# Four of twelve heads' score moves issued by GpSimd from the fourth chunk on

## The chip, the cores and the metric

The kernel runs on one core of one Trainium2 chip. That core has five engines that work side by side, each on its own list of instructions in a fixed order: TensorE (PE in the profile, with its weight loads as PEld), VectorE (DVE), ScalarE (ACT), GpSimd (POOL) and SyncE (SP). An instruction that has to wait holds up all that stand behind it on its engine. DMAs are issued by an instruction of SyncE, GpSimd or ScalarE and then move data on their own. The metric is the device time of one execution in microseconds; the median of several executions is compared.

## The reference

Attention with four batches, twelve heads, 448 rows and 64 columns per head, in which the scores of the twelve heads are mixed with one another before the softmax and once more after it; then two dense layers with an ELU between them; then two dense layers with a softmax gate and a layer norm between them.

```
scores = scale * np.matmul(q, k.transpose(0, 1, 3, 2))
scores = np.einsum('bhij,hg->bgij', scores, w_pre)
scores = scores - np.max(scores, axis=-1, keepdims=True)
attn = np.exp(scores)
attn = attn / (np.sum(attn, axis=-1, keepdims=True) + 1e-09)
attn = np.einsum('bhij,hg->bgij', attn, w_post)
return np.matmul(attn, v).astype(np.float32)          # -> x, 1792 x 768
...
h = x @ w_in                                          # 768 -> 2048
g = np.where(h > 0.0, h, alpha * (np.exp(np.minimum(h, 0.0)) - 1.0))
return (g @ w_out).astype(np.float32)                 # 2048 -> 768
...
h = x @ w_in                                          # 768 -> 1024
sm = e / (np.sum(e, axis=-1, keepdims=True) + 1e-09)
solu = h * sm
ln = (solu - mu) / np.sqrt(var + 1e-06) * g_ln
return (ln @ w_out).astype(np.float32)                # 1024 -> 768
```

## The kernel before

**Attention** is cut into 17 chunks of query rows (numbered 0 to 16), counted in groups of ten rows: 4, 8, 12, 12 and 9 groups in the first batch, 12, 12, 12 and 9 in the others. Two neighbouring groups make a unit (the last of a nine-group chunk has one group), numbered through all chunks; units 88 to 92 lie in the last chunk, among the first work of the dense layers.

For each chunk, `add_score` makes the raw scores: q and k tiles are multiplied two heads at a time on TensorE into PSUM (`sc`, line 445), and ScalarE or VectorE copies each head's scores into one of eight SBUF buffers `sev` (`evac`, line 451). In `sev` a partition is a query row. The mix over heads contracts over the head index, so heads and rows have to stand on the partitions together: a DMA per head, the *move* (`move`, issued through the helper `dma`, line 402), spreads the rows of `sev` into the tile `sp` at a stride of thirteen partitions. A chunk has thirteen moves, one for each of heads 0 to 10 and two half ones for head 11. There are two `sp` tiles, used in turn by the chunks.

When all thirteen moves of a chunk have landed, its units can be mixed: `pm` (line 515) is four matmuls by `w_pre` for each of the unit's groups, the maxima (`st`, line 520) are on VectorE, the exponentials with their sums (`e`, line 525) on ScalarE, then two small operations on VectorE (lines 529 and 532) give the reciprocals. `wr` (line 536, on GpSimd mostly, else on VectorE) multiplies them into the weights of the second mix, which is `po` (line 548): 32 matmuls for each group, with `e` as the stationary operand, so the scores come out transposed. `at` (line 556) copies them to SBUF, `av` (line 597) multiplies by v, `x` (line 604) copies out of PSUM, and a store puts it in DRAM as `xs`. The score making of chunk c + 1 goes between the units of chunk c. In the background the weights of the first dense layers, which arrive as float64 bits, are decoded (`kst`, lines 635 to 652, stored as `w1s`).

At the **handover** to the dense layers, the loads of x (`xst`, line 221, from `xs`), their split into a high and a low fp32r part (cast `xh`, line 225, and subtraction `xl`, line 230) and the split of the first weights (`wy`, lines 693 and 696) stand on the same engines as the last chunk's units. After it come the dense layers (`h`, line 258, and on).

**What sets the order.** Every step of attention is an `op` with a rank (the time it is wanted), the steps it depends on, the buffers it takes and frees, and the engines that may run it with a cost in microseconds on each: `act=.54, dve=.62` lets the planner choose between ScalarE and VectorE. `schedule` goes through the ops in order of time: for each engine it takes the ready op that can start first, keeps that engine's clock, and writes the instruction out. So the costs and the engines of one op change the planned times of all that follow, and with them the order on every engine. A move is planned to land 3.5 us after its end (`lag=3.5`). On the chip the planned times play no part; only the order on each engine and the waits between them stay.

In the kernel before, a move costs .78 on SyncE, may also go to ScalarE in chunks 0 and 1 (`act=.78`), and to GpSimd in chunks 1 and 2 (`pool=1.1`). From chunk 3 on all moves are SyncE's, which also issues the loads of q, k and v, the stores of `xs`, the traffic of the weight decoding and the loads of x.

Of the kernel before, what the change touches and what calls it, by code (L numbers as in the profile page):

```python
# [64 lines left out]
def kernel(ctx: ExitStack, tc: tile.TileContext, qa, kt, vt, wpre, wpost,  # L65
# [223 lines left out]
    def op(rank, emit, deps=(), new=(), uses=(), more=0.0, lag=None, **us):  # L289

        o = Op()
        o.rank, o.emit, o.deps, o.new, o.us, o.more, o.lag = rank, emit, [d for d in deps if d is not None], new, us, more, lag
        for b in chain(new, uses):
            b.users.append(o)
        ops.append(o)
        return o
# [61 lines left out]
    def copier(e):  # L358
        return nc.scalar.copy if e == "act" else nc.vector.tensor_copy
# [15 lines left out]
    for u in range(NU):  # L375
# [4 lines left out]
        c = units[u][0]  # L380
        n = u - first[c]
# [15 lines left out]
    kt_t, kb, q_t, qb_, sp_t, sp_op, pre_op, e_t = {}, {}, {}, {}, {}, {}, {}, {}  # L397
# [3 lines left out]
    def dma(out, in_, e="sp"):  # L401
        {"act": nc.scalar, "pool": nc.gpsimd, "sp": nc.sync}[e].dma_start(out=out, in_=in_)
# [27 lines left out]
    def add_score(c, h):  # L430

        b, _, G = CH[c]
        n = 5 * G
        ring = ("sc", "po", "pm")[h // 2 % 3] if c == 0 else "sc"
        scb, svb = [Buf(ring) for _ in range(2)], [Buf("sev") for _ in range(2)]
        r = t_sc[c, h]
        key = "sc", c, h

        def mm(e):
            T[key] = [pools["ps_" + ring].tile([128, 512], F32, tag=ring, name="sc") for _ in range(2)]  # L440
            q, k = q_t[c, h // 6], kt_t[b, h]
            for x in range(2):
                for i in range(2):
                    sl = slice(64 * i, 64 * i + 64)
                    nc.tensor.matmul(T[key][i][64 * x:64 * x + 64, :S], q[sl, h % 6 // 2, 64 * x:64 * x + 64], k[sl, :],  # L445
                                     start=True, stop=True)

        def evac(e, i):
            t = T["sv", c, h + i] = (k0.tile([128, S], F32, name=f"s0_{h + i}") if c == 0 else
                                     sev_p.tile([128, S], F32, tag="sev", name="sev"))  # L450
            copier(e)(t, T[key][i][:, :S])

        def move(e, i, p, r0, r1):
            if c not in sp_t:
                sp_t[c] = sp_t[c - 2]
            dma(sp_t[c][p:p + 13 * (r1 - r0 - 1) + 1:13, 0:G, :], T["sv", c, h + i][r0 * G:r1 * G], e)

        o1 = op(r, mm, [k_op[b, h], q_op[c, h // 6]], scb, [qb_[c, h // 6], kb[b, h]], pe=SC)
        for i in range(2):
            sv = [] if c == 0 else [svb[i]]  # L460
            o2 = sc_ev[c, h + i] = op(r + .9 + .1 * i, lambda e, i=i: evac(e, i), [o1], sv, [scb[i]], act=.54, dve=.62)
            for n, to in enumerate([(h + i, 0, 10)] if h + i < 11 else [(11, 0, 5), (64, 5, 10)]):
                sp_op.setdefault(c, []).append(op(r + 2 + .2 * i + .1 * n, lambda e, i=i, to=to: move(e, i, *to), [o2], [spb_[c]], sv, lag=3.5, sp=.78, **({"act": .78} if c < 2 else {}), **({"pool": 1.1} if 0 < c < 3 else {})))

    spb_ = {c: Buf(f"sp{(NC - c) % 2}") for c in range(NC)}
    o = op(7.0, lambda e: dma(wpre_t, wpre), sp=.5)
# [18 lines left out]
    for c in range(NC):  # L485
        b = CH[c][0]
        if c == HEAD[b]:
            for h in range(0, NH, 2):
                add_k(b, h)
        for hf in range(2):  # L490
            add_q(c, hf)
        for h in range(0, NH, 2):
            add_score(c, h)
# [81 lines left out]
    for c in range(NC):  # L575
# [12 lines left out]
        for n in range(2):  # L588
            r = t_av[c, n]
# [388 lines left out]
```

## Time and profile before

| | us |
|---|---|
| median of 3 runs | 1119.38 |
| lowest, highest | 1118.16, 1119.91 |
| profiled execution | 1116.97 |
| its span, first to last instruction | 1115.2 |

Its mean granted clock of TensorE is 0.992 of the full one. Busy shares of the span: TensorE 96% (1075.3 us), VectorE 65%, ScalarE 45%, GpSimd 22%. The rows come from one profiled execution, from whose start all times are counted. A matmul count stands for single instructions. "[0.88 <-DMA xs<-x]" says that the engine sat idle for 0.88 us just before, and what ended that by the trace: where a wait is for several DMAs, the one named is not always the one meant. SPq is the queue of DMA issues on SyncE; the duration there is that of the issuing, not of the transfer.

### The profile page before, as it was taken

How to read it: one execution, taken by the hardware profiler on the slowest of the kernel's cores; microseconds unless marked ns; L12 is line 12 of the kernel's file. 1: busy time of each engine (PE TensorE's matmuls, PEld its weight loads, DVE VectorE, ACT ScalarE, POOL GpSimd, SP SyncE). 2: the span in 40 equal slices, each digit the busy share in tenths (PEclk: the TensorE clock that was granted, in tenths of full speed). 3: DMA queues.
4: the chain of work that ended last, by engine and by line, in shares of the span. 5: the costliest groups of instructions: out<-in, count | busy, mean ns of one | idle time of the engine just before them, and what ended most of it. 6: DMA issues, size and time to landing. Idle time of an engine off the chain costs nothing. (4 is left out here: it accounts for less than half of the span.)

```text
span 1115.2 us, 29836 instructions
## 1 busy us (share of the span) xinstructions
PE 1075.3 (96%) x12520; PEld 903.6 (81%) x12520; DVE 727.4 (65%) x1404; ACT 502.5 (45%) x1069; POOL 241.3 (22%) x249
## 2 busy tenths in 40 slices
PE   7889999999998899999999999999999999999998
PEld 2557677667665798898988999999989899898988
DVE  5577677777676647688878887878854553443532
ACT  3466666666665445433333343333431343333422
POOL 3111001011012323444434434343422000000000
PEclk9999999999999899999999999999999999999999
DMA  7775775775744334142434242324162600000001
GB/s 220 192 216 157 227 214 180 229 215 171 219 146 159 119 98 132 63 145 95 170 95 162 84 138 88 127 67 157 30 218 103 245 29 15 29 15 29 22 22 43
DMA packets 80315, 141.76 MB, mean 127 GB/s; under 512 B 20847, under 2 KB 60003, under 8 KB 80181
## 3 DMA queue, kind: packets, MB, share of 16 engines
q1 hardware_dynamic: 78605, 137.02, 38.7%
q8 instruction: 98, 1.61, 0.6%
q10 hardware_dynamic: 1112, 1.73, 0.5%
q0 software_dynamic: 464, 1.11, 0.4%
q14 instruction: 36, 0.29, 0.1%
HBM read 75.96 MB, written 25.17 MB: 91 GB/s over the span
## 5 line engine op out<-in xcount | busy, mean ns | idle before, releaser
L520 DVE TENSOR_REDUCE st<-pm 128x1 f32<-128x448 f32 (+1 forms) x184 | 109.2, 616 | 76.9 <-PE pm L515 76.2
L548 PEld LDWEIGHTS po<-wr,e 60*64 60x64 f32 x5760 | 119.7, 137 | 39.1 <-issue 28.7
L525 ACT ACTIVATE e<-pm,st 128x448 f32<-128x448 f32 (+1 forms) x184 | 115.9, 634 | 74.2 <-DVE st L520 54.6
L750 PE MATMUL o<-gh,woh 128*128 128x448 f32 x384 | 142.2, 370 | 5.8 <-DVE x L766 3.7
L750 PE MATMUL o<-glo,woh 128*128 128x448 f32 x384 | 140.7, 366 | 0.0
L750 PE MATMUL o<-gh,wol 128*128 128x448 f32 x384 | 140.3, 365 | 0.0
L271 POOL TENSOR_TENSOR glo<-g,gh 128x448 fp32r<-128x448 f32 x64 | 83.6, 1307 | 231.5 <-issue 134.3
L548 PE MATMUL po<-wr,e 60*64 60x60 f32 x5760 | 124.9, 221 | 3.7 <-DVE at L556 1.5
L445 PE MATMUL sc<-kt,q 64*64 64x448 f32 x816 | 117.0, 556 | 10.0 <-DMA kt<-in_kt_dram 4.4
L515 PE MATMUL pm<-sp,wpre_t 64*64 64x448 f32 x720 | 110.7, 566 | 13.8 <-ACT e L525 6.1
L893 PE MATMUL o<-w,lh 128*128 128x384 f32 x448 | 120.3, 340 | 0.0
L846 PE MATMUL h<-w,x2h 128*128 128x512 f32 x336 | 107.7, 395 | 0.0
L766 DVE TENSOR_TENSOR x<-x,o 128x448 f32<-128x448 f32 x168 | 101.3, 610 | 8.6 <-PE o L750 8.6
L258 PE MATMUL h<-xh,wih 128*128 128x448 f32 x288 | 105.5, 366 | 0.0
L258 PE MATMUL h<-xh,wil 128*128 128x448 f32 x288 | 105.0, 365 | 0.0
L258 PE MATMUL h<-xl,wih 128*128 128x448 f32 x288 | 104.8, 364 | 0.0
L536 POOL TENSOR_TENSOR wr<-wpost_t,st 128x120 f32<-128x120 f32 (+1 forms) x92 | 36.1, 392 | 298.7 <-DVE st L532 214.2
L266 ACT ACTIVATE t<-t 128x448 f32<-128x448 f32 x64 | 37.0, 578 | 134.2 <-DVE t L265 134.2
L597 PEld LDWEIGHTS av<-at,v 128*64 128x64 f32 x1632 | 75.6, 137 | 19.3 <-ACT e L525 7.8
L597 PE MATMUL av<-at,v 128*64 128x120 f32 (+3 forms) x1632 | 83.0, 258 | 2.9 <-issue 2.3
L750 PEld LDWEIGHTS o<-gh,woh 128*128 128x128 f32 x384 | 72.5, 189 | 15.1 <-DVE x L766 7.0
L893 PEld LDWEIGHTS o<-w,lh 128*128 128x128 f32 x448 | 81.7, 188 | 0.6
(96 smaller groups left out, 1936.3 us busy)
## 6 DMA issues: line engine op xcount, KB each, us to landing
sp<-sev SPq DMA_DIRECT2D x117, 210.0 KB
ws<-in_wi_dram SPq DMA_DIRECT2D x33, 512.0 KB
ws<-in_wo_dram SPq DMA_DIRECT2D x21, 512.0 KB
sp<-sev SPq DMA_DIRECT2D x44, 157.5 KB
q<-in_qa_dram SPq DMA_DIRECT2D x34, 192.0 KB
v<-in_vt_dram SPq DMA_DIRECT2D x24, 256.0 KB
w2s<-ws SPq DMA_DIRECT2D x12, 512.0 KB
ws<-in_wo_dram SPq DMA_DIRECT2D x16, 384.0 KB
```

The lines of the kernel that those rows point to most:

```text
L258: nc.tensor.matmul(ps[:, :S], a[:, kc * FG + ft * 128:kc * FG + (ft + 1) * 128], x[:, kc, :], start=kc == 0 and n == 0, stop=kc == ECH - 1 ...
L271: nc.gpsimd.tensor_tensor(glo, g, f(gh), ALU.subtract)
L445: nc.tensor.matmul(T[key][i][64 * x:64 * x + 64, :S], q[sl, h % 6 // 2, 64 * x:64 * x + 64], k[sl, :], start=True, stop=True)
L515: nc.tensor.matmul(ps_t[u][r][64 * s:64 * s + 64, :S], wpre_t[sl, :], sp_t[c][sl, g + s, :], start=True, stop=True)
L520: nc.vector.tensor_reduce(out=st_t[u][:P, r:r + 1], in_=ps_t[u][r][:P, :S], op=ALU.max, axis=AX.X, negate=True)
L525: nc.scalar.activation(out=t[:P], in_=ps_t[u][r][:P, :S], func=AF.Exp, bias=st[:P, r:r + 1], scale=1.0, accum_out=st[:P, 2 + r:3 + r])
L548: nc.tensor.matmul(out[:, :, 5 * r:5 * r + 5], e_t[u, r][sl, j:j + 64], wr_t[u][sl, r].rearrange("p (g a) -> p g a", a=5), start=True, sto ...
L597: nc.tensor.matmul(ps[64 * k:64 * k + 64, i, :], v_t[CH[c][0]][:, 6 * n + 2 * i + k, q, :], at_t[c][:, q, 6 * n + 2 * i + k, :w], start=q ...
L750: nc.tensor.matmul(ps[:, :S], a[:, ft * DM + e * 128:ft * DM + (e + 1) * 128], x, start=n == 0, stop=n == 5)
L766: nc.vector.tensor_tensor(x1[tb][:, e, :], x1[tb][:, e, :], ps[:, :S], ALU.add)
L846: nc.tensor.matmul(ps[:, hf * 512:hf * 512 + 512], a[:, k, :], w, start=n == 0, stop=n == 3 * ECH - 1)
L893: nc.tensor.matmul(ps[:, :384], a[:, k, :], w, start=n == 0, stop=n == 3 * FC - 1)
```

## The change

The `op` that plans a move gets other engines: from chunk 3 on, heads 1, 4, 7 and 10 (those with `(h + i) % 3 == 1`) may only be issued by GpSimd, at a planned cost of 1.0; all others keep what they had.

```diff
@@ -460,7 +460,8 @@
             for n, to in enumerate([(h + i, 0, 10)] if h + i < 11 else [(11, 0, 5), (64, 5, 10)]):
-                sp_op.setdefault(c, []).append(op(r + 2 + .2 * i + .1 * n, lambda e, i=i, to=to: move(e, i, *to), [o2], [spb_[c]], sv, lag=3.5, sp=.78, **({"act": .78} if c < 2 else {}), **({"pool": 1.1} if 0 < c < 3 else {})))
+                sp_op.setdefault(c, []).append(op(r + 2 + .2 * i + .1 * n, lambda e, i=i, to=to: move(e, i, *to), [o2], [spb_[c]], sv, lag=3.5, **({"pool": 1.0} if c > 2 and (h + i) % 3 == 1 else
+                              {"sp": .78, **({"act": .78} if c < 2 else {}), **({"pool": 1.1} if 0 < c < 3 else {})})))
```

That is four moves in each of 14 chunks, 56 in all. The same bytes go the same way; what differs is the engine that issues these DMAs and, through the planner, the order on all engines. Lines behind the edit stand one further down in the changed kernel (536 is 537 there).

SyncE, in the score making of chunk 4 (nine groups), where moves stand ahead of the next loads of q. Before:

```order
L402 DMA xs<-x 128x3x80
L402 DMA sp<-sev 10x9x448 x8
L402 DMA q<-in_qa_dram 128x384
L402 DMA sp<-sev 10x9x448 x2
L402 DMA q<-in_qa_dram 128x384
L402 DMA sp<-sev 10x9x448
L402 DMA sp<-sev 5x9x448
```

After:

```order
L402 DMA xs<-x 128x3x80
L402 DMA sp<-sev 10x9x448 x5
L402 DMA q<-in_qa_dram 128x384
L402 DMA sp<-sev 10x9x448 x2
L402 DMA q<-in_qa_dram 128x384
L402 DMA w1s<-kst 128x192
L402 DMA sp<-sev 5x9x448 x2
```

Eight moves ahead of the first q have become five.

GpSimd, from the last of its moves before on. Before, `wr` follows on `wr` (64 partitions where the unit has one group), chunk after chunk:

```order
L402 DMA sp<-sev 10x12x448
L536 TENSOR_TENSOR wr<-wpost_t,st 128x120 x19
L536 TENSOR_TENSOR wr<-wpost_t,st 64x120
L536 TENSOR_TENSOR wr<-wpost_t,st 128x120 x22
L536 TENSOR_TENSOR wr<-wpost_t,st 64x120
```

After, here around the moves of chunk 4 and the first of chunk 5:

```order
L402 DMA sp<-sev 10x9x448
L537 TENSOR_TENSOR wr<-wpost_t,st 128x120
L402 DMA sp<-sev 10x9x448
L537 TENSOR_TENSOR wr<-wpost_t,st 128x120
L402 DMA sp<-sev 10x9x448
L537 TENSOR_TENSOR wr<-wpost_t,st 128x120
L402 DMA sp<-sev 10x9x448
L537 TENSOR_TENSOR wr<-wpost_t,st 128x120 x4
L402 DMA sp<-sev 10x12x448 x2
L537 TENSOR_TENSOR wr<-wpost_t,st 128x120 x2
```

Moves now stand between the `wr`, each ahead of one or more of them; GpSimd has 62 moves instead of six.

VectorE, at the handover, around the maxima (line 520, 521 in the changed kernel) of units 88 and 89. Before:

```order
L556 COPY at<-po 128x48x10
L225 CAST xh<-xst 128x896 x2
L529 TENSOR_SCALAR st<-st 128x2
L520 TENSOR_REDUCE st<-pm 128x1
L532 RECIPROCAL st<-st 128x2
L520 TENSOR_REDUCE st<-pm 128x1
L693 CAST wih<-wy 128x512
L230 TENSOR_TENSOR xl<-xst,xh 128x896
L696 TENSOR_TENSOR wil<-wy,wih 128x512
L520 TENSOR_REDUCE st<-pm 128x1 x2
```

After:

```order
L225 CAST xh<-xst 128x896
L230 TENSOR_TENSOR xl<-xst,xh 128x896
L530 TENSOR_SCALAR st<-st 128x2
L521 TENSOR_REDUCE st<-pm 128x1
L533 RECIPROCAL st<-st 128x2
L521 TENSOR_REDUCE st<-pm 128x1
L694 CAST wih<-wy 128x512
L225 CAST xh<-xst 128x896 x2
L521 TENSOR_REDUCE st<-pm 128x1 x2
```

Ahead of the first pair of maxima, two casts of x have become one cast and one subtraction; between the two pairs, a cast and two subtractions have become three casts. On ScalarE the cast of x that stood ahead of the exponentials of unit 88 (line 525) has gone to VectorE.

## Rows read from the trace of the kernel before

**Rows 1.** Stretches: start and end, length, busy by engine (instructions), granted clock, DMA share, GB/s

```profile
core 0: us, PE busy (x) PEld busy (x) DVE busy (x) ACT busy (x) POOL busy (x), PEclk, DMA share, GB/s
80.00:350.00 270.00, 262.53 (x6901) 188.13 (x6902) 190.51 (x486) 175.15 (x469) 27.99 (x72) 1.00 0.64 190
355.96:372.33 16.37, 10.49 (x190) 7.56 (x191) 13.24 (x22) 7.33 (x18) 8.82 (x7) 0.69 0.39 132
359.30:369.50 10.20, 7.66 (x139) 4.95 (x142) 8.78 (x14) 5.23 (x13) 5.09 (x4) 0.50 0.44 144
```

**Rows 2.** Timeline of TensorE: start, length, operation, [idle before, what ended it]

```profile
69.98 1.16 PE L515 MATMUL pm<-sp,wpre_t 64*64 64x448 f32 x5 [0.88 <-DMA xs<-x]
...
80.93 0.98 PE L445 MATMUL sc<-kt,q 64*64 64x448 f32 x8 [2.83 <-DMA q<-in_qa_dram]
...
135.15 1.06 PE L515 MATMUL pm<-sp,wpre_t 64*64 64x448 f32 x5 [0.69 <-DMA xs<-x]
...
284.79 1.18 PE L515 MATMUL pm<-sp,wpre_t 64*64 64x448 f32 x5 [0.77 <-DMA q<-in_qa_dram]
```

**Rows 3.** Timeline of SyncE's DMA issues, 61 to 78 us

```profile
61.55 2.43 SPq L402 DMA_DIRECT2D sp<-sev  x3
...
69.76 6.84 SPq L402 DMA_DIRECT2D sp<-sev  x8
76.66 0.49 SPq L402 DMA_DIRECT2D q<-in_qa_dram  x1
```

**Rows 4.** Tile sp, 80 to 350 us: durations (ns, min/median/max), starts

```profile
L402 SPq DMA_DIRECT2D sp<-sev x159: 742/756/1738, 79.6 to 339.5; - x159
```

**Rows 5.** Handover: timelines of SyncE, VectorE, ScalarE, TensorE; last row tile xst

```profile
349.91 0.37 SPq L221 DMA_DIRECT2D xst<-xs  x1
...
355.63 0.63 DVE L225 CAST xh<-xst 128x896 fp32r<-128x896 f32 x1 [2.36 <-issue]
357.56 1.38 DVE L225 CAST xh<-xst 128x896 fp32r<-128x896 f32 x1 [1.31 <-DMA xst<-xs]
...
358.93 0.61 DVE L520 TENSOR_REDUCE st<-pm 128x1 f32<-128x448 f32 x1
...
360.06 0.41 DVE L693 CAST wih<-wy 128x512 fp32r<-128x512 f32 x1
...
364.95 1.14 DVE L520 TENSOR_REDUCE st<-pm 128x1 f32<-128x448 f32 x2
...
359.15 0.94 ACT L225 CAST xh<-xst 128x896 fp32r<-128x896 f32 x1 [4.64 <-DMA xst<-xs]
...
360.77 1.02 PE L515 MATMUL pm<-sp,wpre_t 64*64 64x448 f32 x3 [4.81 <-ACT e L525]
...
L230 DVE TENSOR_TENSOR xl<-xst,xh x4: 1092/1202/2152, 360.4 to 408.9; 128x896 fp32r<-128x896 f32 x4
```

**Rows 6.** Line 402 on GpSimd, whole span: durations (ns), time to landing

```profile
L402 POOL DMA_DIRECT2D sp<-sev x6: 582/622/761, 13.3 to 40.2; - x6
...
DMA to landing us min/median/max: 4.6/6.9/9.2
```

**Rows 7.** Tiles wr and sev, 80 to 350 us: durations; who waited (us, times)

```profile
L536 POOL TENSOR_TENSOR wr<-wpost_t,st x72: 381/388/437, 84.6 to 347.2; 128x120 f32<-128x120 f32 x69, 64x120 f32<-64x120 f32 x3
...
  PEld po L548: 1.2, 3
...
L451 DVE COPY sev<-sc x40: 608/624/625, 82.0 to 334.8; 128x448 f32<-128x448 f32 x40
```

**Rows 8.** Timeline of TensorE, 86 to 89 us: three blocks in turn

```profile
86.14 0.98 PE L515 MATMUL pm<-sp,wpre_t 64*64 64x448 f32 x8
86.94 1.11 PE L548 MATMUL po<-wr,e 60*64 60x60 f32 x64
87.87 0.94 PE L445 MATMUL sc<-kt,q 64*64 64x448 f32 x8
```

**Rows 9.** Timeline of GpSimd and VectorE, 25 to 27 us

```profile
25.57 0.62 POOL L402 DMA_DIRECT2D sp<-sev  x1 [2.00 <-DVE sev L451]
...
25.84 0.62 DVE L451 COPY sev<-sc 128x448 f32<-128x448 f32 x1
```

## Prediction

> **What bounds the kernel now.** I read a table of stretches first [rows 1], for how full TensorE is where the edit reaches. The edit touches attention chunks 3 to 16, roughly from 60 us to the handover to the MoE near 378 us. From 80 to 350 us TensorE is busy for 262.53 of 270.00 us, so all its idle time there is 7.47 us. At the handover, from 355.96 to 372.33 us, it is busy for 10.49 of 16.37 us, and around 359.30 to 369.50 us the granted clock is 0.50, the 1.2 GHz level, after an idle stretch of 4.81 us. After 380 us nothing is edited, so what is won before can only come from TensorE's idle time, from its clock, or from matmuls that overlap better.
>
> Next, TensorE's waits in order of time [rows 2]. Before 80.93 us it waits 2.83 us for a load of q. The first matmuls on a chunk's spread scores (line 515) wait 0.88, 0.69 and 0.77 us at 69.98, 135.15 and 284.79 us. A DMA is named in each, though not the same one, and the place is the start of a chunk, so I take the late landing of its last moves as the cause. SyncE's queue shows why [rows 3]: eight moves in 6.84 us, 0.855 us each, stand ahead of that q, which leaves at 76.66 us. Here SyncE limits itself: one move occupies it for 0.756 us in the median [rows 4].
>
> Last, the handover [rows 5]. The first load of x leaves at 349.91 us. VectorE's first cast of it starts at 355.63, its second at 357.56 after a wait for a landing, and only then come the maxima of unit 88 (358.93). ScalarE's cast of the third piece waits until 359.15 us with the next exponentials behind it. TensorE stops at 360.77 - 4.81 = 355.96 and goes on at 360.77 us. The next maxima start at 364.95, after more MoE preparation on VectorE.
>
> **The change, part by part.**
>
> *56 moves leave SyncE.* Heads 1, 4, 7 and 10 of 14 chunks. At 0.756 us each [rows 4], SyncE is free of 56 x 0.756 = 42 us of issuing. That is work off the path. On the path is only what waited for SyncE. For the q load: eight moves ahead become five, so it can leave 3 x 0.855 = 2.57 us earlier [rows 3], and of the 2.83 us some 0.3 stay: 2.5 us gained. For the three chunk starts (0.88 + 0.69 + 0.77 = 2.34 us) four of 13 moves of a chunk leave the queue, but the evacuations ahead of the moves and the landings are as they were, and loads of k move up into the gaps: I take half, 1.2 us. Sum 3.7 us; bounds 0 (another wait ends at the same time) and 7.47 + 0.88 = 8.35 us (all idle time from the start of chunk 3 on) [rows 1, 2].
>
> *56 moves come to GpSimd.* GpSimd's six moves of before took 0.58 to 0.76 us each, landing after 6.9 us in the median [rows 6]. For SyncE's moves no landing is shown; the wait at 69.98 us ends 6.0 us after SyncE's last move of that chunk (61.55 + 2.43 = 63.98) [rows 2, 3], about the same. So a move is not slower to arrive, as far as this trace tells. GpSimd works for 28 us of the 270 [rows 1], and 56 x 0.62 = 35 us more fit. What can cost is order: GpSimd takes its instructions in turn, and behind a move that waits for its evacuation stands `wr` (line 536, 0.388 us [rows 7]), which the 32 matmuls of `po` (line 548) wait for. I compared, for each of the 56, how much TensorE work stands between the scores that feed the move and the `po` that needs the `wr` behind it. At the tightest place it is pm, sc, po, pm, sc: by starts and lengths of such blocks 0.80 + 0.94 + 0.93 + 0.80 + 0.94 = 4.4 us [rows 8]. The chain against it is one evacuation of at most 0.63 us [rows 7], two moves (0.62 each) and `wr`: 2.3 us, about 3.2 with some 0.2 us for each of the hand-overs. So it hides, with 1 us to spare, and 13 of the 62 moves on GpSimd have 5.5 us or less. Cost between 0 and 13 x 0.62 = 8.1 us (each tight place shows one whole move); I take 1.5, near the lower end, since the chain fits.
>
> A DMA issued by GpSimd could also be held up by VectorE. The trace: a move issued at 25.57 us, while VectorE copied out of PSUM from 25.84 us on, took 0.62 us, and the shortest of the six took 0.58 [rows 6, 9]. So copies out of PSUM cost a move 0.04 us at most. The Trainium skill (SBUF — State Buffer, section SBUF: two separate sides) warns of this change: while VectorE runs an fp32 SBUF-to-SBUF copy, GpSimd can't write descriptors, and a DMA of 620 ns took 3100. By that, each move that meets such an op would cost about 2.5 us (an estimate from that page); only the few small ops on `kst` are of the kind here, and no run shown has such a meeting.
>
> *The planner's order changes.* Since moves are planned at other times, all engines' orders shift a little. In chunks 4 to 16 I see swaps of neighbours on TensorE, which I cost at nothing: the same matmuls, each with a filled queue behind it. At the handover the order is better for the waits named above. VectorE now does one cast and one subtraction of x ahead of unit 88's maxima, not two casts that wait for landings, and ScalarE has no cast of x ahead of unit 88's exponentials. The first cast still starts some 5.7 us after the first load, whose place (behind the last pm of chunk 15) hasn't changed; the subtraction takes 1.09 to 2.15 us [rows 5]. So unit 88's maxima start at about 355.63 + 0.63..1.38 + 1.09..2.15 = 357.4 to 359.2, against 358.93: 1.5 us earlier to 0.3 later; and ScalarE then goes straight on where it was held by its cast until 360.09. Between unit 88's and unit 89's maxima stand a cast of weights (0.41) and two casts of x, 3.2 us at the most; before it was 4.9 us from that cast to the maxima (360.06 to 364.95): 1.7 us earlier, and more with the first. The subtraction that frees the buffer for the fifth load also comes earlier. I take 3.5 us, bounds 0 and 9.7: all idle time, 16.37 - 10.49 = 5.9, and half of the 7.66 us at half clock, 3.8 [rows 1].
>
> *Sum.* -3.7 + 1.5 - 3.5 = -5.7 us. Against the profiled execution's own 1116.97 us (span 1115.2 and 1.8 around it): 1111.3. The timed median is 1119.38, 2.4 above the profiled one, which I take as the same offset for both kernels: 1119.38 - 5.7 = **1113.7 us**.
>
> **The rivals.**
>
> *Nothing of it is on the path* (1119.4, give or take 2). The waits for q and for the chunk starts go, but what is next (evacuation buffers, PSUM slots) ends as late, and the handover falls out as before because the loads of x land when they did. For: idle time is 2.8% of the stretch (7.47 of 270), and TensorE's blocks are dense [rows 1]. Against: eight moves back to back ahead of a q that TensorE waits for [rows 2, 3]. The Trainium skill (DMA: Bandwidth & Descriptors, Issuing engines are not separate DMA queues) leans this way: several issuers save only the time to issue, which is usually small.
>
> *GpSimd's turn makes `wr` late: slower.* Place: a `wr` behind a move whose evacuation is late. It decides where the evacuation ends over 1.8 us later than the chain of 3.2 us supposes. If the 13 tight places each show one move, 8.1 us, and the handover gains nothing: 1119.38 - 3.7 + 8.1 = 1123.8. For: evacuations stand in ScalarE's and VectorE's own order and need a free one of eight buffers. Against: weights for `po` waited for `wr` for 1.2 us in three places before [rows 7], and the planner knows the moves.
>
> *VectorE holds up the issue on GpSimd.* A move that meets a copy is lengthened by a whole copy, 0.63 us [rows 7]; at the 13 tight places 8.2 us on top of the forecast: 1113.7 + 8.2 = 1121.9. Against it stands the 0.62 us of [rows 6].
>
> *The handover clears.* If TensorE's stop is short enough that the clock doesn't fall, all 9.7 us come: 1119.38 - 3.7 + 1.5 - 9.7 = 1107.5. For: both blocking casts are gone from ScalarE's path. Against: the first x lands no earlier.
>
> **How the numbers follow.** Forecast 0.53, nothing on the path 0.21, late `wr` 0.12, held issue 0.04, handover clears 0.10. About 0.2% (2.2 us) is what a measurement of this kernel can tell from no change. The forecast's own range is 1109 to 1117.1: faster. Faster is 0.53 + 0.10, less 0.02 of the forecast's edge, plus 0.01 of the second: 0.62. Same: 0.18 of the second and 0.02: 0.20. Slower: 0.12 + 0.04 + 0.02 = 0.18. For 8 in 10 the range takes the forecast, the second, most of the handover case and half of the slower cases: 1107 to 1123.
>
> **What would show it.** The q wait near 81 us down from 2.83 to under 0.5; waits at chunk starts halved; nine of 13 moves a chunk on SyncE, 62 in all on GpSimd at about 0.6 us each. At the handover, TensorE's stop under 3.5 us where 4.81 stood, maxima of unit 89 some 2 to 4 us earlier against the last pm of chunk 15, and less time at the 1.2 GHz level. It is wrong if TensorE waits for `wr` in sum over 3 us, if GpSimd's moves take over 1 us, or if a stop of the same length stands at the handover.

## The result, and the profile after

The changed kernel takes 1131.15 us in the median of 6 runs (1125.17 to 1136.76), the kernel before, beside it, 1118.22 (1113.31 to 1119.91). The ratio is 1.0125, with an interval of 1.0097 to 1.0154: **some 14 us slower**. The prediction said 1113.7 us, faster. The profiled execution of the changed kernel took 1133.48 us (span 1131.7, 16.5 more than before).

**Where along the way.** The reciprocals of the units are marks that both traces have (units are counted from 0 here; by that count the last chunk's are 87 to 91, not 88 to 92 as the description of the kernel has it). Against before they come later by 4.5 us at unit 16, 16.5 at unit 40, 24.8 at unit 56 and 28.6 at unit 84. Then comes the handover, and at the first dense matmul (line 258) it is 16.9 us. Timelines of VectorE and TensorE, start and length, first of before, then of after:

```profile
342.29 0.17 DVE L532 RECIPROCAL st<-st 128x2 f32<-128x2 f32 x1
...
378.76 0.47 PE L258 MATMUL h<-xh,wih 128*128 128x448 f32 x1
```

```profile
370.92 0.17 DVE L533 RECIPROCAL st<-st 128x2 f32<-128x2 f32 x1
...
395.68 0.47 PE L258 MATMUL h<-xh,wih 128*128 128x448 f32 x1
```

From the one mark to the other it was 36.5 us and is 24.8: the handover gives back 11.7 us. The order shown ahead of the prediction does it: unit 88's maxima follow unit 87's after 2.9 us where it was 7.4, unit 89's follow unit 88's after 4.1 where it was 6.0 (lines further down), and the clock stays up.

```profile
core 0: us, PE busy (x) PEld busy (x) DVE busy (x) ACT busy (x) POOL busy (x), PEclk, DMA share, GB/s
84.00:377.00 293.00, 270.73 (x6957) 189.93 (x6958) 195.59 (x495) 174.29 (x467) 57.78 (x120) 0.99 0.65 175
376.67:392.00 15.33, 12.80 (x342) 8.29 (x342) 14.26 (x29) 10.90 (x30) 8.33 (x9) 1.00 0.70 235
```

(Stretches of after: start and end, length, busy by engine, granted clock.) The second row answers to the handover of [rows 1]: the clock is 1.00 where it was 0.69. The first answers to the long stretch there: TensorE's idle time has gone from 7.47 of 270 us to 22.27 of 293.

**What TensorE waits for now**, from 60 to 400 us: engine, line, what ended the wait; us in all, times, longest. Before:

```profile
PE pm L515 <- ACT e L525: 6.1, 3, 4.8
PE sc L445 <- DMA q<-in_qa_dram: 3.1, 2, 2.8
PE av L597 <- issue: 1.6, 1, 1.6
PE pm L515 <- DMA xs<-x: 1.6, 2, 0.9
...
PE po L548 <- issue: 1.3, 3, 0.8
```

After:

```profile
PE po L549 <- issue: 11.5, 7, 3.1
PE pm L516 <- ACT e L526: 4.8, 5, 1.9
PE sc L445 <- ACT sev L451: 4.1, 6, 1.3
PE po L549 <- DVE at L557: 2.4, 2, 1.5
PE av L598 <- issue: 1.9, 1, 1.9
PE po L549 <- ACT at L557: 1.5, 6, 0.6
PE sc L445 <- DMA q<-in_qa_dram: 0.2, 1, 0.2
PE pm L516 <- issue: 0.2, 1, 0.2
```

The waits that the change was to remove are gone (q, and the starts of chunks). Two kinds are new: for work of ScalarE (`sev`, `e`, `at`), and stops that the trace puts down to no semaphore at all ("issue"): 13.6 us where there were 3.2. What ScalarE in turn waits for, first before, then after, same columns:

```profile
ACT sev L451 <- DMA sp<-sev: 0.4, 1, 0.4
```

```profile
ACT sev L451 <- DMA sp<-sev: 23.8, 11, 3.8
```

An evacuation of scores waits for a *move* to land: its buffer is still being read. One such case, in the timelines of GpSimd and ScalarE after:

```profile
152.04 0.62 POOL L402 DMA_DIRECT2D sp<-sev  x1 [1.25 <-DVE sev L451]
...
157.04 0.20 ACT L526 ACTIVATION_READ_ACCUMULATOR e<-pm,st 128x1 f32 x1
160.35 0.97 ACT L451 COPY sev<-sc 128x448 f32<-128x448 f32 x2 [3.11 <-DMA sp<-sev]
```

The move of 152.04 us lands at 160.27 by the increments of its semaphore, 8.2 us later. The evacuation that gets its buffer is only the fifth behind the one that the move reads; there are eight buffers. The addresses in the built program say that this is no accident. Before, a buffer came round after 8.0 evacuations in the mean. In the changed kernel, from the fourth chunk on, the tile pool gives the buffer of a move on GpSimd to an evacuation 4.4 later (2 to 7), that of a move on SyncE 9.8 later (8 to 12). The planner reckons with eight in turn. Worked out so from the addresses and the semaphores' increments in the trace, 26 of the 54 evacuations that take over a buffer from GpSimd start within 0.35 us of the landing, and none of the 105 that take one over from SyncE.

GpSimd's moves themselves look as predicted: duration in ns (min/median/max), and time to landing in us.

```profile
L402 POOL DMA_DIRECT2D sp<-sev x62: 580/619/767, 14.2 to 364.1; - x62
...
DMA to landing us min/median/max: 2.7/5.7/10.1
```

### The profile page after: what moved, and what is told of

The parts are those of the page before. It is cut to its first block, busy times and chain, and to the rows that moved or that the text cites. A ratio compares the mean times of both kernels' runs of the same rounds, so it can differ in the third digit from the quotient of the medians.

```text
span 1131.7 us, 29904 instructions
## 1 busy us (share of the span) xinstructions
PE 1082.7 (96%) x12520; PEld 902.1 (80%) x12520; DVE 730.5 (65%) x1410; ACT 499.7 (44%) x1062; POOL 274.3 (24%) x306
## 5 line engine op out<-in xcount | busy, mean ns | idle before, releaser
L445 PE MATMUL sc<-kt,q 64*64 64x448 f32 x816 | 122.3, 572 | 10.4 <-ACT sev L451 5.3
L451 ACT COPY sev<-sc 128x448 f32<-128x448 f32 x127 | 64.4, 535 | 50.9 <-DMA sp<-sev 23.8
L557 DVE COPY at<-po 128x480 f32<-128x480 f32 (+1 forms) x124 | 77.3, 647 | 12.9 <-PE po L549 12.7
```

## The experiments

Two things are in the way, then: the buffers that come round too soon (S), and something that makes TensorE stop without a semaphore. A third suspect is the order that the planner now writes on all engines (O). GpSimd as issuer (I) could be at the root of the second.

All ratios below are to the kernel before, run on the same chip beside each.

**1. Buffers in turn.** Tags make the buffers rotate; all engines have the same instructions in the same order as in the changed kernel.

```diff
-sev_p.tile([128, S], F32, tag="sev", name="sev"))
+sev_p.tile([128, S], F32, tag=f"sev{next(sev_n) % SB}", name="sev", bufs=1))
```

> The changed kernel, with one thing different: the eight buffers of the scores (sev) are taken strictly in turn. In the changed kernel the pool hands them out in another way: by the addresses in the built program, the buffer of a move issued by GpSimd goes to an evacuation only 4.4 evacuations later (2 to 7), that of a move issued by SyncE 9.5 later, where it was 8 for all before. Instructions and their order on all engines are the same. Theory S (short reuse: evacuations wait for the landing of a move that has just been issued, 20.7 us of such waits on ScalarE and 3.2 on VectorE in the trace): the waits go; attention ends some 25 us earlier than in the changed kernel while the handover keeps the 12 us that it gave back there: 1100 to 1110 us. Theory I (moves on GpSimd land late, or hold its queue): no change, 1128 to 1134. Theory O (the order that the planner now writes on the other engines is worse): no change, 1128 to 1134.

Measured: 1119.16 us, ratio 1.0030 (1.0004 to 1.0056). Against the changed kernel's 1.0125 that is 0.0095, 10.6 us; the intervals of both leave 6 to 15. ScalarE's wait for landings is gone:

```profile
ACT sev L451 <- DMA sp<-sev: 0.3, 1, 0.3
```

By the addresses, 1 of 52 evacuations still starts at the landing of a move of GpSimd, where it was 26 of 54. So S is real, but it isn't all: the time falls between what S and I expected. The rest stands in TensorE's own waits of this run:

```profile
PE po L549 <- issue: 17.2, 10, 3.2
PE av L598 <- issue: 2.8, 2, 2.6
...
PE pm L516 <- issue: 0.4, 2, 0.2
```

**2. The control**: the same edit in the kernel before.

> The kernel before, with the eight buffers of the scores taken strictly in turn; there the reuse was 8 evacuations later in the mean already (4 to 11). A control for the first run: under all theories 1115 to 1121 us, no change that can be measured.

Measured: 1117.80 us, ratio 1.0023 (1.0004 to 1.0042). To take the buffers in turn brings nothing by itself and, if anything, costs 2.6 us (0.4 to 4.7); the gain of the first run is the gain over the short reuse.

**3. The order without the issuer.** The plan of the changed kernel, with the moves written to SyncE's queue.

```diff
-            dma(sp_t[c][...], T["sv", c, h + i][r0 * G:r1 * G], e)
+            dma(sp_t[c][...], T["sv", c, h + i][r0 * G:r1 * G], "sp" if c > 2 else e)
```

> The changed kernel's plan and its order on TensorE, VectorE and ScalarE, but the 56 moves are issued by SyncE, in the places where the plan puts them. The pool then hands the buffers out 7.7 evacuations later. Theory S: fast, 1103 to 1114 us (the handover's 12 us and no short reuse). Theory I: fast as well, 1103 to 1114. Theory O: as slow as the changed kernel, 1128 to 1134.

Measured: 1110.33 us, ratio 0.9953 (0.9934 to 0.9971), 5.3 us **faster than before**. O falls. The way through the handover is the changed kernel's, 24.7 us (timelines of VectorE and TensorE, the same marks as above):

```profile
343.82 0.17 DVE L533 RECIPROCAL st<-st 128x2 f32<-128x2 f32 x1
...
368.55 0.47 PE L258 MATMUL h<-xh,wih 128*128 128x448 f32 x1
```

**4. The short reuse without GpSimd.** As run 3, with the buffers handed out in the changed kernel's sequence, written as a list of 192 digits.

```diff
-sev_p.tile([128, S], F32, tag="sev", name="sev"))
+sev_p.tile([128, S], F32, tag=f"sev{next(sev_n)}", name="sev", bufs=1))
```

> As the third run (all moves on SyncE, the changed kernel's order), but with the buffers handed out in the very sequence of the changed kernel, 4.4 evacuations later for the heads in question. Theory S: as slow as the changed kernel or slower, since these moves also queue behind others on SyncE: 1126 to 1145 us. Theory I: as fast as the third run, 1103 to 1114. Theory O: 1128 to 1134, and the third run too.

Measured: 1117.59 us, ratio 1.0018 (1.0001 to 1.0034): 7.3 us slower than run 3, between what I and S expected. The waits are there again, though GpSimd issues none of these moves:

```profile
ACT sev L451 <- DMA sp<-sev: 23.0, 11, 3.9
```

The four kernels (after, 1, 3, 4) differ in two things, the issuer and the sequence of the buffers. Short reuse costs 10.6 us with the moves on GpSimd and 7.3 with them on SyncE. GpSimd as issuer costs (1.0030 - 0.9953) x 1117 = 8.6 us with the buffers long in use and (1.0125 - 1.0018) x 1117 = 12.0 with the short reuse. The 8.6 compares buffers strictly in turn (run 1) with the pool's own sequence (run 3, 8.0 in the mean); with the 2.6 us of run 2 taken off it is 6.0, and the short reuse is 13.2 in place of 10.6. S and I are both true, and each was expected to be alone.

**5. ScalarE as issuer**, buffers in turn, to see what in "GpSimd" it is.

```diff
-            dma(sp_t[c][...], T["sv", c, h + i][r0 * G:r1 * G], e)
+            dma(sp_t[c][...], T["sv", c, h + i][r0 * G:r1 * G], "act" if c > 2 and e == "pool" else e)
```

> The first run (changed kernel, buffers taken strictly in turn), but the 56 moves are issued by ScalarE in the places of the plan where GpSimd issues them. In the first run's trace TensorE stands still for 25.4 us in sum, in stops of over 0.35 us in which it waits for no semaphore, where the third run (all moves on SyncE) has 9.2 and the kernel before 5.5; nearly all of the long ones end 1.3 to 1.7 us after a 16 KB packet of the instruction queue. Theory P (two queues with moves at a time delay the instruction fetches, whoever issues): the sum of these stops stays at 17 to 30 us. Theory G (it is GpSimd's own DMAs, which have other packets): the sum falls to 5 to 12 us. In both cases 56 x 0.78 = 44 us of issuing more on ScalarE may cost time of its own, so the total says little: P 1116 to 1130, G 1106 to 1122.

Measured: 1142.35 us, ratio 1.0214 (1.0189 to 1.0239). The time is outside both expectations, since ScalarE's own queue is too full for it (TensorE waits 12.5 us for moves in this trace). The stops, which the run was made for, sum to 9.0 us, and the view has:

```profile
PE po L549 <- issue: 4.3, 4, 2.6
```

A second queue with moves doesn't make them. That speaks for G, on a kernel that is slower for another reason.

**6. Half the dose**: of the 56, heads 4 and 10 go to SyncE, buffers in turn.

```diff
+            dma(sp_t[c][...], T["sv", c, h + i][r0 * G:r1 * G], "sp" if c > 2 and h + i in (4, 10) else e)
```

> The first run with half the dose: heads 1 and 7 of the 14 chunks on GpSimd (28 moves), heads 4 and 10 in the same places of the plan on SyncE; buffers strictly in turn. Theory P or G (the cost of GpSimd's moves is the instruction fetches that they delay, move by move): stops between the third run's 9.2 and the first one's 25.4 us, 1112 to 1117 us. Rival (the cost arises once, by the mere use of the second queue): as the first run, 1117 to 1122.

Measured: 1114.33 us, ratio 0.9974 (0.9950 to 0.9998). Run 3 is 0.9953 and run 1 1.0030, so it lies between, below the middle of 0.9992. The rival is out. That the cost grows move by move isn't shown by it, though: the interval takes in run 3, run 2's 0.0023 for buffers in turn would make up the difference, and the stops, expected above run 3's, are 5.9 us by the profile's rows against 6.0 there.

**7. The handover alone**, in the kernel before.

```diff
-[ws], sp=.5, more=1.0)
+[ws], sp=.5, more=2.5)
```

> The kernel before with one number of the plan changed: the loads of x at the handover are planned to land 2.5 us after their issue, not 1.0. All moves stay on SyncE, the order up to the handover is as before; there unit 88's maxima stand ahead of all but no casts of x on VectorE, and its exponentials ahead of ScalarE's cast. In the changed kernel and in three runs the way from unit 84's reciprocal to the first dense matmul is 24.7 to 24.9 us, in the kernel before 36.5. Theory: that is the order of the handover alone: 24 to 28 us here too, and 1104 to 1110 us. Rival (it is what the attention before it leaves behind, loads done earlier or buffers free earlier): 33 to 37 us, and 1114 to 1120.

Measured: 1113.28 us, ratio 0.9955 (0.9937 to 0.9973), 5 us faster. The way through the handover is 29.2 us by these rows, against 36.5:

```profile
351.06 0.17 DVE L532 RECIPROCAL st<-st 128x2 f32<-128x2 f32 x1
...
380.30 0.47 PE L258 MATMUL h<-xh,wih 128*128 128x448 f32 x1
```

The order there is worth as much as run 3 gains, without any change in attention. Its way is 1 us longer than expected, and the time 3 us: this order isn't quite the changed kernel's, and TensorE still stops once for 2.30 us.

**8 to 11. More traces**, since the stops differ from one execution to another (runs 2 and 3: 6.5 and 9.2 us by the measure of the expectations): run 1 twice more, the changed kernel and run 3 once more each.

> The first run once more, for a second trace. The stops of TensorE of over 0.35 us without a semaphore (60 to 400 us) summed to 25.4 us there, against 5.5 to 12.6 us in the five traces in which SyncE or ScalarE issues the 56 moves (kernel before and runs 2, 3, 5 and 7: 5.5, 6.5, 9.2, 9.0, 12.6). Theory G (GpSimd's moves delay the instruction fetches): 15 to 27 us again. Rival V (the sum differs from run to run whoever issues, and the first trace was a bad one): 6 to 14 us.

> A third trace of the same kernel. Theory G: 15 to 27 us of such stops. Rival V: 6 to 14 us.

> The changed kernel once more, for a second trace: its first had 17.5 us of such stops. Theory G: 13 to 25 us. Rival V: 6 to 14 us.

> The third run once more (same order, all moves on SyncE): its first trace had 9.2 us of such stops. Theory G: 5 to 12 us. Rival V: anything from 6 to 20 us.

Measured (stops of over 0.35 us, as in the expectations): 16.3 and 17.9 us for run 1, 16.7 for the changed kernel, as G said; 12.9 for run 3, just over G's 12. In the rows that the profile itself gives ("issue" in TensorE's waits, 60 to 400 us, summed):

| moves of the fourth chunk on, issued by | us without a semaphore, trace by trace | mean |
|---|---|---|
| SyncE (before, 2, 7, 3, 11, 4) | 3.2, 4.0, 8.8, 6.0, 8.9, 7.1 | 6.3 |
| SyncE and ScalarE (5) | 4.3 | |
| 28 of them by GpSimd (6) | 5.9 | |
| 56 of them by GpSimd (1, 8, 9, after, 10) | 20.4, 13.1, 13.9, 13.6, 12.8 | 14.8 |

The two groups of several traces don't overlap, and their means differ by 8.4 us, within what GpSimd as issuer costs in time (6.0 to 12.0). Within a group they spread by 6 to 8 us.

What these stops are can be read from single records. The trace has the packets of a queue of kind "instruction", 98 of 16 KB in an execution, 61 to 65 of them from 60 to 400 us. Of the 50 stops of over 1 us of idle time in the 14 traces (before, after and the twelve runs), all end 1.2 to 1.8 us after the end of such a packet; that window covers 11% of the time. A second sign is stronger: when TensorE's records (matmuls, weight loads, semaphore instructions) are numbered in order of time, all 50 stops end at the same place of a block of 256, at number 193 beyond a multiple of 256; with the shorter stops, 129 of the 132 us lie there. The kernel before has 25,245 such records, and 98 blocks of 256 are 25,088. So a packet is a block of TensorE's instructions, and TensorE stands still until its next block has come. That blocks come later because of GpSimd's moves is what runs 1 and 3 and the table say. The packets themselves take no longer, 1.1 us in the mean in either group; they start later, 1.3 to 1.6 us in the mean after TensorE has begun the block ahead, against 1.1 to 1.3 with SyncE. What holds their start up isn't shown.

**12. Other DMAs on GpSimd**: as run 3, with 64 loads of q, k and v on GpSimd in place of the moves.

```diff
-            dma(q_t[c, hf], qa[c, :, 3 * hf:3 * hf + 3])
+            dma(q_t[c, hf], qa[c, :, 3 * hf:3 * hf + 3], "pool" if c > 2 else "sp")
...
-            dma(kt_t[b, h], kt[b, h // 2], e)
+            dma(kt_t[b, h], kt[b, h // 2], "pool" if b else e)
```

> The third run (changed kernel's order, all moves on SyncE), but from the fourth chunk on (k and v: from the second batch on) the loads of q, k and v, 64 in all and 192 to 256 KB each, are issued by GpSimd in the places where the plan puts them on SyncE. In the row of waits of TensorE that end by nothing that the trace shows, 60 to 400 us, the traces with 56 moves on GpSimd have 12.8 to 20.4 us, those without 3.2 to 8.9. Theory G1 (whatever GpSimd issues delays the instruction fetches): 12 to 20 us here, and 1116 to 1126 us. Theory G2 (it is the moves as GpSimd writes them: 5376 bytes a packet where SyncE's have 1792): 4 to 9 us here, and 1106 to 1114 us. Waits of GpSimd for a free buffer, with weights for the second mix behind them, could add some us in both and would be named so in TensorE's waits.

Measured: 1113.34 us, ratio 0.9950 (0.9930 to 0.9970), the same as run 3's 0.9953. Its waits:

```profile
PE po L549 <- issue: 7.8, 9, 1.9
...
PE av L598 <- issue: 1.8, 2, 1.5
...
PE pm L516 <- issue: 0.9, 1, 0.9
```

10.5 us lie between the two groups and settle nothing; the time says more: these loads on GpSimd cost nothing that can be seen, though a gain from SyncE's shorter queue could hide a small cost. The size of the packets alone, as G2 had it, isn't it either: GpSimd's loads have packets of 3072 to 5376 bytes as well. Another number sets the moves apart: from 60 to 400 us, packets of 1792 bytes on SyncE's queue take 93 ns in the mean in every trace without a move on GpSimd there, 95 with 28 of them and 100 to 102 with 56; run 12, where the queue has lost the loads, has 90.

What is special about the moves **stays open**. One trait can be read: a move posts 11 increments on its semaphore when SyncE issues it (6 for a half one) and 16 when GpSimd does. The Trainium skill (DMA: Bandwidth & Descriptors, Why a DMA increments its semaphore by 16 and not by 1) explains the 11 and 6: a transfer runs on the largest number of engines, up to 16, that divides the slowest dimension of both its sides, so ten for ten rows and five for five, on SyncE always the lowest-numbered of the 16, and what is missing to 16 is written at once, as one more increment. By the same page of the Trainium skill, all 16 engines post for a DMA of GpSimd, and the engines that carry it are taken in turn from all 16. The counts agree with that. If the instructions come through one of the six engines that SyncE's moves never use, then GpSimd's moves hold them up, ScalarE's don't (run 5), and loads over all 16 engines change nothing (run 12). No record here names the engine of a packet, so this is an argument, not a finding.

## Why the prediction was wrong

Taken from the ratios, the 14.0 us of the change are: the order, -5.3 (run 3 against before); GpSimd as issuer, +8.6 (run 1 against 3); short reuse, +10.6 (after against 1). The last two share their 19.2 differently, 6.0 and 13.2, with run 2's 2.6 us taken into account.

**56 moves leave SyncE (-3.7).** In the rows the waits are gone: TensorE's 2.83 us for q at 80.93 [rows 2] is now

```profile
82.97 0.98 PE L445 MATMUL sc<-kt,q 64*64 64x448 f32 x8 [0.23 <-DMA q<-in_qa_dram]
```

and no wait for a move at a chunk's start is left in the table of after. TensorE was late itself by then, though; in run 1, which isn't yet late at unit 16, q's wait is 1.0 us, in run 3 2.4. So some 1.5 of the 2.5 us for q were there.

**56 moves come to GpSimd (+1.5, bounds 0 and 8.1). This is the step that failed.** Each thing in it that was costed came out as said: 0.62 us a move, as in [rows 6]; weights of `po` waited 0.4 us for `wr` in all, where 1.2 had been [rows 7]; the longest move took 0.77 us, so VectorE held up none. But the step asked only what a move costs GpSimd's queue. It did not ask what else hangs on *when and by whom* a move is issued: the pool hands out the buffers by it, and instructions come by DMA as well, through a queue of their own (q8 below). The text even named the free buffer among eight, in the rival of the late `wr`, and took the eight for granted. The addresses in the built program would have shown 4.4 ahead of any run. The price of the two together was 19.2 us, more than double the upper bound. The second part of it could not have been read ahead: no row of before shows a DMA on GpSimd in the stretch in question, and 3.2 us of "issue" in TensorE's waits gave no hint of what doubles it.

The move "not slower to arrive" was a shade wrong as well: worked out from the semaphores' increments, SyncE's moves land 4.9 us after issue in the mean before, and 5.8 after; GpSimd's take 5.7. The six early moves on GpSimd (6.9) had been no measure for SyncE's.

**The planner's order at the handover (-3.5, bounds 0 and 9.7).** Right in mechanism, mis-sized: 11.7 us by the marks in after, 11.8 and 11.6 in the traces of runs 3 and 1, above the upper bound. VectorE does not wait for a load there at all. Timelines of VectorE before, then of SyncE and VectorE after:

```profile
351.49 0.62 DVE L520 TENSOR_REDUCE st<-pm 128x1 f32<-128x448 f32 x1 [0.22 <-PE pm L515]
```

```profile
375.46 0.37 SPq L221 DMA_DIRECT2D xst<-xs  x1
...
378.08 0.62 DVE L521 TENSOR_REDUCE st<-pm 128x1 f32<-128x448 f32 x1 [0.32 <-PE pm L516]
...
379.21 0.62 DVE L225 CAST xh<-xst 128x896 fp32r<-128x896 f32 x1
379.87 1.09 DVE L230 TENSOR_TENSOR xl<-xst,xh 128x896 fp32r<-128x896 f32 x1
...
380.94 0.62 DVE L521 TENSOR_REDUCE st<-pm 128x1 f32<-128x448 f32 x1
...
385.00 1.14 DVE L521 TENSOR_REDUCE st<-pm 128x1 f32<-128x448 f32 x2
```

The prediction let the cast start as long after its load as before, 5.7 us. Here the first load leaves at 375.46 us and the cast starts 3.8 us later, right behind unit 87's maxima; unit 88's follow at 380.94 where it would put them at 375.46 + 5.7 + 0.62 + 1.09 = 382.9 or later. TensorE's stop of 4.81 us [rows 5] is gone, and with it the 1.2 GHz stretch: this was the mechanism of the fourth rival, at a chance of 0.10. It held at the handover; the time that went with it, 1107.5 us, did not come.

Of these 11.7 us only 5.3 are left in run 3's time. In the traces its attention is 1.5 and 10.6 us later than before's at unit 84, that of run 2 5.0, much of it stops without a semaphore, 6.0 and 8.9 against before's 3.2. How much of the difference is order and how much is the spread of executions isn't settled.

**The rivals.** The slower one had the right sign and a wrong place: `wr` was not late (0.4 us of waits, as above). Its "evacuations need a free one of eight buffers" was the real place, under another mechanism. The rival that the move does not matter failed both ways. The Trainium skill's rule on VectorE (SBUF — State Buffer, SBUF: two separate sides), which the prediction weighed, did not show up: no move of the 62 took over 0.77 us.

Run 3 is the version to keep: 1110.33 us, 0.47% faster than before (0.29 to 0.66), with every move where it was.

## What to carry to other kernels

When a transfer is given to another issuer, look at what is handed out by its issue, above all the buffers: read from the built program how many uses later each comes round, and hold that against the landing time, not against the number of buffers. A planner that assumes buffers in turn needs a pool that hands them out in turn. And a stop of TensorE in the middle of a block, with no semaphore, is a cost to count in every trace beside its waits; it can come from DMAs that no instruction waits for.

## What the runs showed of the hardware

TensorE runs out of instructions in this kernel: 3 to 9 us per execution when SyncE issues the moves, 13 to 20 when GpSimd issues 56 of them, each stop of over 1 us ending 1.2 to 1.8 us after a 16 KB packet of the instruction queue and at the same place of a block of 256 instructions (50 of 50). It may be a part of why executions of one kernel differ by up to 10 us: run 1's three traces have 20.4, 13.1 and 13.9 us of it and took 1126.66, 1117.26 and 1118.28 us.

The same 56 moves take more time of the DMA engines when GpSimd issues them. From the queues on the profile's page (packets, MB, share of 16 engines' span), before and after:

```profile
q1 hardware_dynamic: 78605, 137.02, 38.7%
q8 instruction: 98, 1.61, 0.6%
...
q0 software_dynamic: 464, 1.11, 0.4%
```

```profile
q1 hardware_dynamic: 71805, 125.84, 35.8%
q0 software_dynamic: 4688, 12.31, 4.3%
```

By the shares, the moves gave back 0.387 x 1115.2 - 0.358 x 1131.7 = 26.4 us of all 16 engines on SyncE's queue and took 0.043 x 1131.7 - 0.004 x 1115.2 = 44.2 us on GpSimd's, for the same 11.2 MB. That is not 1.7 times as much for the moves alone, since what stayed on SyncE's queue became slower (93 to 101 ns for 1792 bytes, as above). Packet by packet it is 1.2 times: from 60 to 400 us GpSimd's packets of 5376 bytes take 335 ns in the mean in the changed kernel, and three of the 1792-byte packets that ScalarE makes of the same moves in run 5 take 3 x 91 = 273.
